# Product operands moved by 64 bytes within each partition of the on-chip memory, in a fused attention, expert and gated-unit kernel

## The chip, the core and the metric

The kernel runs on one core of one Trainium2 chip. Its metric is the device time of one execution in microseconds. Three runs of the kernel before gave 1065.58, 1065.71 and 1065.73 us; the median is 1065.71 us. A core has a matrix engine (TensorE: PE for its matmuls, PEld for its weight loads), a vector engine (VectorE, DVE), a scalar engine (ScalarE, ACT), a third elementwise engine (GpSimd, POOL) and queues for transfers (SP). All of them work on SBUF, a memory of 128 partitions; a tile takes the same byte addresses in each partition. Matmul results go to PSUM, another memory.

## The reference

Three layers follow each other: an attention with a coarse and a local part, a mixture of eight experts with balanced gates, and a gated unit.

```python
x = (out_up + out_local)                       # attention, to 1152 tokens x 512
P = balanced(exp(x @ w_gate))                  # eight rounds of row and column normalisation
for e in range(8):
    out += P[:, e:e+1] * (np.maximum(x @ w1[e], 0.0) @ w2[e])     # w1[e] 512x1024, w2[e] 1024x512
y = ((out @ w_a) * (out @ w_b)) @ w_out        # w_a, w_b 512x1536, w_out 1536x512
```

## The kernel before

Every float32 operand of a large matmul is split into a high part and a low part, and each product is a sum of three matmuls: high by high, high by low, low by high. A matmul instruction has a stationary operand, up to 128 columns that a weight load (LDWEIGHTS) brings into the array, and a moving operand that streams through it. All matmuls go through `mm` (lines 59 and 60): its second argument is the stationary operand, its third the moving one.

The experts' work is cut into 16 units (an expert's half of the hidden width, 512 columns), the gated unit's into six (256 columns). The 1152 tokens are worked on in two chunks, 512 tokens (four tiles of 128) and 640 tokens (five tiles). Units 0 and 1 are worked on in blocks of 384 tokens, before the chunks begin. Each unit has two layers:

- First layer (`g_plain`, `g_chunk`, `g_whole`): the stationary operand is a block of weights from the ring `w` (13 blocks, `new_block`), the moving operand is the activations: `xh` and `xl`, or their combinations `Th` and `Tl`, with 256, 320 or 384 columns. Its results, evicted from PSUM and split, are the product operands `gh` and `gl`.
- Second layer (`o_mm`, line 526): the stationary operand is 128 columns of `gh` or `gl`, the moving operand is a block of second weights from the same ring, 512 columns. A token tile takes 12 matmuls for an expert unit, six for a gated unit. The result is added to `acc`.

Three weight blocks of unit 1's second layer do not lie in the ring but in spare tiles, `we` (line 1301).

The two layers alternate on PE: `phase` (line 825) runs the first layer of one chunk, and puts the second layer's tiles of the other chunk between its steps. The instruction order of each engine is fixed when the program is built.

The place of a tile in a partition comes from the order and sizes of the pools. Pools `const`, `xp`, `gp`, `wr` and `stg` stand one behind the other from below: `P` and small tiles, `xh`, `xl`, a tile `line` that nothing reads or writes (line 86), `acc`, then `gh0`, `gh1`, `gl0`, `gl1` (pool `gp`; used by units 0 and 1, and by chunk 1 afterwards), then the ring, then the staging tiles. From above come `spare`, `tp` (with `Th`, `Tl`, and the unused tile `linet`) and `g0p`, which holds chunk 0's product operands `gh_00`, `gh_01`, `gl_00`, `gl_01` and an unused tile `lineg` (line 1464). Each slice that a matmul reads starts a multiple of 256 bytes behind its tile's start.

The start of these tiles in a partition, modulo 256 bytes, in the built program:

| tiles | read by PE as | start modulo 256 |
|---|---|---|
| `xh`, `xl`, `Th`, `Tl` | moving, first layer | 192 |
| ring blocks `w` | stationary in the first layer, moving in the second | 0 |
| `gh`, `gl` in `gp` (units 0 and 1, chunk 1) | stationary, second layer | 0 |
| `gh_0`, `gl_0` in `g0p` (chunk 0) | stationary, second layer | 0 |
| `we` (three blocks of unit 1) | moving, second layer | 224 |
| `acc` | stationary in transposes; source of the stores to the output | 0 |

Of the kernel before, what the change touches and what calls it, by code (L numbers as in the profile page):

```python
# [8 lines left out]
F32 = mybir.dt.float32  # L9
# [10 lines left out]
def attn_moe_glu_kernel(  # L20
# [42 lines left out]
    xp = ctx.enter_context(tc.tile_pool(name="xp", bufs=1))  # L63
    gp = ctx.enter_context(tc.tile_pool(name="gp", bufs=1))
# [18 lines left out]
    P = P_[:, 0:NT, 0:E]  # L83
    xh = xp.tile([128, KT, N], F32R, name="xh")
    xl = xp.tile([128, KT, N], F32R, name="xl")
    xp.tile([128, 16], F32, name="line")
    acc = [xp.tile([128, DM], F32, name=f"acc{t}") for t in range(NT)]


# [377 lines left out]


    GP = [[gp.tile([128, 4, TB], F32R, tag=f"{x}{n}", name=f"{x}{n}") for n in range(2)] for x in ("gh", "gl")]

    def g_part(u, ps, b, f, kts):

        cols = slice(b * TB, (b + 1) * TB)
        for kt in kts:
            w = u.w[f // 2, kt // 2]
            o = (kt % 2) * 256 + (f % 2) * 128
            a_h, a_l = w.hi[:, o:o + 128], w.lo[:, o:o + 128]
            parts = (a_h, xh), (a_l, xh), (a_h, xl)
            for k, (l, r) in enumerate(parts):
                mm(ps, l, r[:, kt, cols], kt == 0 and k == 0, kt == KT - 1 and k == 2)  # L480
        M.pe += 0.52 * len(kts)
# [24 lines left out]
    def g_plain(u, n, b, f, mid, ps=None, full=False):  # L506

        gh, gl = GP[0][n], GP[1][n]
        if ps is None:
# [31 lines left out]
    def o_moe(u, gh, gl, t, tt, mid=None, first=False):  # L541
        if u.e > 0:
            while gens[0] is not None:
                side_step()
        ps = o_mm(u, gh, gl, t)
        if mid:
            if closed:
                pump(0.0)
            mid()
        if not first:  # L550
            pump()
        a = acc[tt]
        if u.e == 0:
            if u.hf == 0 and closed:
                nc.scalar.copy(out=a, in_=ps)
                act(0.65)
                return
            if u.hf == 0:
                nc.vector.tensor_copy(out=a, in_=ps)
            else:  # L560
                nc.vector.tensor_tensor(out=a, in0=ps, in1=a, op=ALU.add)
        else:
            if u.e == 1 and u.hf == 0:
                nc.scalar.mul(out=a, in_=a, mul=P[:, tt, 0:1])
                act(0.65)
            nc.vector.scalar_tensor_tensor(  # L566
                out=a, in0=ps, scalar=P[:, tt, u.e:u.e + 1], in1=a, op0=ALU.mult, op1=ALU.add
            )
        dve(0.76)
        if first:  # L570
            pump()
# [693 lines left out]
    with tc.manual_schedule():  # L1265
# [134 lines left out]
        for b in range(NB):  # L1400
# [23 lines left out]
            for n in range(2):  # L1424
# [5 lines left out]
                for f in range(4):  # L1430
# [7 lines left out]
                lambda n=n, t=t, b=b: o_moe(  # L1438
                    units[n], *([G[n][:, f] for f in range(4)] for G in GP), t, b * per + t, mid)
                for t in range(per)  # L1440
# [11 lines left out]
        g0p = ctx.enter_context(tc.tile_pool(name="g0p", bufs=1, side="right"))  # L1452
# [8 lines left out]
        for x, G in (("h", GH), ("l", GL)):  # L1461
            t = [g0p.tile([128, 2, 512], F32R, tag=f"g{x}_0{n}", name=f"g{x}_0{n}") for n in range(2)]
            G.append([t[f // 2][:, f % 2] for f in range(4)])
        g0p.tile([128, 48], F32, tag="lineg", name="lineg")

        def o_tile(u, c, t):
            tt = TILES[c][t]
# [112 lines left out]
```

## Time and profile before

| what | value |
|---|---|
| median of three runs | 1065.71 us |
| the profiled execution's own time | 1065.72 us |
| its span, first to last instruction | 1063.9 us |
| PE busy | 1055.9 us (99%) |
| weight loads busy | 964.9 us (91%) |
| VectorE, ScalarE, GpSimd busy | 773.9, 456.9, 521.4 us |
| granted TensorE clock, mean | 1.000 |

The end of a matmul in the trace is modelled and lies behind the start of the next one, so consecutive records overlap. The distance between two starts is the pace at which PE really goes; a record's duration is longer than that by a nearly fixed amount. In the rows below, a name on the left of the arrow is written, those on the right are read; for a matmul the first of these is the moving operand, the second the stationary one, and numbers of buffers are left out (`gh` stands for all tiles of that kind).

### The profile page before, as it was taken

How to read it: one execution, taken by the hardware profiler on the slowest of the kernel's cores; microseconds unless marked ns; L12 is line 12 of the kernel's file. 1: busy time of each engine (PE TensorE's matmuls, PEld its weight loads, DVE VectorE, ACT ScalarE, POOL GpSimd, SP SyncE). 2: the span in 40 equal slices, each digit the busy share in tenths (PEclk: the TensorE clock that was granted, in tenths of full speed). 3: DMA queues.
4: the chain of work that ended last, by engine and by line, in shares of the span. 5: the costliest groups of instructions: out<-in, count | busy, mean ns of one | idle time of the engine just before them, and what ended most of it. 6: DMA issues, size and time to landing. Idle time of an engine off the chain costs nothing.

```text
span 1063.9 us, 17910 instructions
## 1 busy us (share of the span) xinstructions
PE 1055.9 (99%) x6508; PEld 964.9 (91%) x6508; DVE 773.9 (73%) x1535; ACT 456.9 (43%) x1143; POOL 521.4 (49%) x516
## 2 busy tenths in 40 slices
PE   8999999999999999999999999999999999999998
PEld 7999988998899998999999899999989899999997
DVE  7885638777778887877788787778855576667664
ACT  7764514554445344344534434453443553233221
POOL 4532226544655646455564645556451375355521
PEclk9999999999999999999999999999999999999999
DMA  6743001232313233231323223131322002121002
GB/s 166 172 121 96 14 1 40 70 105 65 117 52 127 78 126 95 82 116 54 127 66 128 101 88 106 64 127 58 117 67 60 21 1 60 60 60 42 20 21 89
DMA packets 81256, 84.50 MB, mean 79 GB/s; under 512 B 35856, under 2 KB 55312, under 8 KB 81168
## 3 DMA queue, kind: packets, MB, share of 16 engines
q1 hardware_dynamic: 79984, 83.07, 25.3%
q8 instruction: 51, 0.84, 0.3%
q10 hardware_dynamic: 1184, 0.30, 0.1%
q14 instruction: 37, 0.30, 0.1%
HBM read 71.54 MB, written 11.80 MB: 78 GB/s over the span
## 4 chain that ended last, share of the span: by engine, by line
PE 74%; DVE 0%; issue 0%
PE g L60 73%; PE g L840 0%; DVE acc L1478 0%; DVE G L705 0%
## 5 line engine op out<-in xcount | busy, mean ns | idle before, releaser
L60 PE MATMUL g<-w,gh 128*128 128x512 f32 x1314 | 408.7, 392 | 0.0
L60 PE MATMUL g<-xh,w 128*128 128x256 f32 (+2 forms) x1536 | 333.3, 301 | 0.2 <-DVE G L705 0.2
L701 POOL TENSOR_TENSOR gl<-G,gh 128x256 fp32r<-128x256 f32 (+1 forms) x208 | 172.7, 839 | 265.3 <-ACT gh L699 259.0
L60 PEld LDWEIGHTS g<-w,gh 128*128 128x128 f32 x1314 | 235.7, 188 | 38.0
L60 PEld LDWEIGHTS g<-xh,w 128*128 128x128 f32 x1536 | 255.0, 189 | 4.9 <-DVE G L705 0.6
L60 PE MATMUL g<-w,gl 128*128 128x512 f32 x657 | 256.2, 390 | 0.0
L60 PE MATMUL g<-xl,w 128*128 128x320 f32 (+2 forms) x768 | 230.4, 300 | 0.0
L138 DVE TENSOR_TENSOR w<-raw,w 128x512 fp32r<-128x512 f32 x135 | 127.4, 954 | 108.4 <-ACT w L137 108.3
L60 PE MATMUL g<-Th,w 128*128 128x320 f32 (+1 forms) x912 | 199.0, 295 | 0.2 <-DVE G L705 0.2
L705 DVE TENSOR_TENSOR G<-g,G 128x256 f32<-128x256 f32 (+1 forms) x380 | 154.6, 447 | 24.2 <-PE g L60 9.3
L697 ACT ACTIVATE G<-G 128x256 f32<-128x256 f32 (+1 forms) x168 | 74.3, 443 | 210.7 <-DVE G L705 210.7
L60 PEld LDWEIGHTS g<-Th,w 128*128 128x128 f32 x912 | 152.3, 188 | 4.8 <-DVE G L705 1.9
L60 PEld LDWEIGHTS g<-xl,w 128*128 128x128 f32 x768 | 144.2, 188 | 3.8
L60 PEld LDWEIGHTS g<-w,gl 128*128 128x128 f32 x657 | 123.5, 188 | 26.6
L60 PE MATMUL g<-Tl,w 128*128 128x256 f32 (+1 forms) x456 | 134.2, 294 | 0.0
L566 DVE SCALAR_TENSOR_TENSOR acc<-g,P,acc 128x512 f32<-128x512 f32 x126 | 93.7, 744 | 51.1 <-PE g L60 45.8
L699 ACT CAST gh<-G 128x256 fp32r<-128x256 f32 (+1 forms) x208 | 90.2, 433 | 91.5 <-DVE G L715 78.1
L137 ACT CAST w<-raw 128x512 fp32r<-128x512 f32 x180 | 107.4, 619 | 48.7 <-POOL raw L268 43.6
L398 POOL TENSOR_TENSOR dec<-dec 128x384 f32<-128x384 f32 x48 | 48.7, 1014 | 96.8 <-DVE dec L395 96.8
L60 PEld LDWEIGHTS g<-Tl,w 128*128 128x128 f32 x456 | 85.7, 188 | 2.8
L138 POOL TENSOR_TENSOR w<-raw,w 128x512 fp32r<-128x512 f32 x45 | 59.3, 1324 | 24.0 <-ACT w L137 24.0
L268 POOL TENSOR_TENSOR s<-raw 128x512 f32<-128x512 f32 x38 | 62.2, 1637 | 3.9 <-DMA raw<-w 3.4
(178 smaller groups left out, 1137.8 us busy)
## 6 DMA issues: line engine op xcount, KB each, us to landing
raw<-in_moe_w_dram SPq DMA_DIRECT2D x128, 256.0 KB
w<-dec SPq DMA_DIRECT2D x48, 192.0 KB
dec<-in_moe_w_a_dram SPq DMA_DIRECT2D x16, 384.0 KB
dec<-in_moe_w_b_dram SPq DMA_DIRECT2D x16, 384.0 KB
dec<-in_moe_w_out_dram SPq DMA_DIRECT2D x16, 384.0 KB
raw<-w SPq DMA_DIRECT2D x48, 128.0 KB
raw<-w SPq DMA_DIRECT2D x12, 256.0 KB
vw<-in_v_dram SPq DMA_DIRECT2D x72, 35.0 KB
```

The source lines that it names most:

```text
L60: nc.tensor.matmul(out=o, lhsT=l, rhs=r, start=start, stop=stop, skip_group_check=not check)
L137: nc.scalar.copy(out=hi, in_=raw)
L138: lows.append(lambda: (low or nc.vector).tensor_tensor(out=lo, in0=raw, in1=hi.bitcast(F32), op=ALU.subtract))
L268: nc.gpsimd.tensor_tensor(out=o(), in0=A(*a), in1=A(*b), op=op)
L398: nc.gpsimd.tensor_tensor(out=tf, in0=tf, in1=mf, op=ALU.add)
L566: nc.vector.scalar_tensor_tensor(out=a, in0=ps, scalar=P[:, tt, u.e:u.e + 1], in1=a, op0=ALU.mult, op1=ALU.add)
L697: nc.scalar.activation(out=src, in_=src, func=AF.Relu)
L699: nc.scalar.copy(out=h, in_=src)
L701: nc.gpsimd.tensor_tensor(out=l, in0=src, in1=h.bitcast(F32), op=ALU.subtract)
L705: nc.vector.tensor_tensor(out=o, in0=bank_, in1=b, op=ALU.add)
```

## The change

Two sizes of unused tiles are changed and one unused tile is added. No instruction is added, removed or moved on any engine, and no wait changes; only places of tiles do.

```diff
@@ pool xp, ahead of acc
-    xp.tile([128, 16], F32, name="line")
+    xp.tile([128, 32], F32, name="line")
@@ pool gp, behind GP
+    gp.tile([128, 48], F32, tag="linep", name="linep")
@@ pool g0p, behind gh_0 and gl_0
-        g0p.tile([128, 48], F32, tag="lineg", name="lineg")
+        g0p.tile([128, 32], F32, tag="lineg", name="lineg")
```

What that does to places, in bytes of a partition (from the two built programs):

| tiles | before | after | modulo 256 |
|---|---|---|---|
| `xh`, `xl`, `Th`, `Tl`, `we` | 18880, 37312, 181696, 195520, 217056 | the same | unchanged |
| `acc0` | 55808 | 55872 | 0 to 64 |
| `gh0`, `gh1`, `gl0`, `gl1` | 74240, 80384, 86528, 92672 | 64 higher | 0 to 64 |
| `gh_00`, `gh_01`, `gl_00`, `gl_01` | 165120, 169216, 173312, 177408 | 64 higher | 0 to 64 |
| `w0` to `w12`, staging tiles | 98816 for `w0` | 256 higher | unchanged, 0 |

## Rows read from the trace of the kernel before

**Rows 1.** The page: span, busy time by engine, granted clock in tenths.

```profile
span 1063.9 us, 17910 instructions
...
PE 1055.9 (99%) x6508; PEld 964.9 (91%) x6508; DVE 773.9 (73%) x1535; ACT 456.9 (43%) x1143; POOL 521.4 (49%) x516
...
PEclk9999999999999999999999999999999999999999
```

**Rows 2.** The chain of waits in order of time: start us, us, what.

```profile
276.59 558.32 PE g L60 x3288
...
852.68 207.58 PE g L60 x1332
...
1060.28 0.69 DVE acc L1478
```

**Rows 3.** Groups by shape on PE, whole span: names, shapes, count, busy, mean ns.

```profile
L60 PE MATMUL g<-w,gh 128*128 128x512 f32 x1314 | 408.7, 392 | 0.0
L60 PE MATMUL g<-w,gl 128*128 128x512 f32 x657 | 256.2, 390 | 0.0
L60 PE MATMUL g<-xh,w 128*128 128x320 f32 x672 | 157.5, 309 | 0.0
L60 PE MATMUL g<-xh,w 128*128 128x256 f32 x672 | 130.6, 281 | 0.2 <-DVE G L705 0.2
...
L60 PE MATMUL g<-xl,w 128*128 128x320 f32 x336 | 103.8, 309 | 0.0
L60 PE MATMUL g<-xl,w 128*128 128x256 f32 x336 | 94.2, 280 | 0.0
...
L60 PE MATMUL g<-we,gh 128*128 128x512 f32 x54 | 17.0, 396 | 0.0
...
L60 PE MATMUL g<-we,gl 128*128 128x512 f32 x27 | 10.7, 396 | 0.0
```

**Rows 4.** Timeline, second-layer tile of chunk 1: start us, us, instruction, count.

```profile
602.45 0.62 PE L60 MATMUL g<-w,gh 128*128 128x512 f32 x2
...
602.90 0.39 PE L60 MATMUL g<-w,gl 128*128 128x512 f32 x1
602.91 0.41 PEld L60 LDWEIGHTS g<-w,gh 128*128 128x128 f32 x2
...
603.81 0.28 PE L60 MATMUL g<-xh,w 128*128 128x256 f32 x1
```

**Rows 5.** Timeline, second-layer tile of chunk 0.

```profile
625.28 0.63 PE L60 MATMUL g<-w,gh 128*128 128x512 f32 x2
...
626.44 0.39 PE L60 MATMUL g<-w,gl 128*128 128x512 f32 x1
...
628.04 0.31 PE L60 MATMUL g<-xh,w 128*128 128x320 f32 x1
```

**Rows 6.** Groups by shape on PE, 1054.7 to 1060 us, the last four tiles.

```profile
L60 PE MATMUL g<-w,gh 128*128 128x512 f32 x16 | 4.9, 389 | 0.0
L60 PE MATMUL g<-w,gl 128*128 128x512 f32 x9 | 3.5, 389 | 0.0
```

**Rows 7.** Timeline, first layer with 320 columns.

```profile
628.18 0.31 PE L60 MATMUL g<-xl,w 128*128 128x320 f32 x1
...
629.50 0.31 PE L60 MATMUL g<-xl,w 128*128 128x320 f32 x1
```

**Rows 8.** Timeline, first layer with 256 columns, at the beginning of a phase.

```profile
646.22 0.28 PE L60 MATMUL g<-xl,w 128*128 128x256 f32 x1
...
647.81 0.63 PE L60 MATMUL g<-w,gh 128*128 128x512 f32 x2
```

**Rows 9.** Timeline, first layer with 256 columns, later in a phase.

```profile
608.41 0.28 PE L60 MATMUL g<-xl,w 128*128 128x256 f32 x1
...
609.36 0.39 PE L60 MATMUL g<-w,gh 128*128 128x512 f32 x1
```

## The prediction, made before the changed kernel ran

> **What bounds the kernel now.** I read the page first: PE is busy for 1055.9 of 1063.9 us, and its clock is granted in full in all forty slices, which is the 2.4 GHz level [rows 1]. The chain of waits says the same in order of time: from 276.59 us it is PE's matmuls and nothing else for 558 us, then, after a short mixed piece, for another 208 us, and the last thing in it is a VectorE add at 1060.28 us [rows 2]. So no wait can be won or lost; what counts is the pace of the matmuls themselves. At 2.4 GHz a matmul of n columns would need n/2.4 ns, and the groups by shape with the timeline show how much longer it takes.
>
> The second layer has 1314 + 657 = 1971 matmuls of 512 columns with a ring block moving, recorded with 392 and 390 ns [rows 3]. A record is longer than the pace. In the settled tile of the timeline six matmuls lie between the starts at 602.45 and 603.81 us, so the pace is 1360/6 = 226.7 ns [rows 4]. The last tiles are settled too, and their records have 389 ns [rows 6]; I use 389.5, since tiles in the middle give 389 or 390. Record minus pace is therefore some 163 ns. 512/2.4 is 213.3 ns, so a settled matmul loses 13.4 ns. In the same timeline the next weight load starts with the matmul (602.90 and 602.91 us) [rows 4]: PE reads two operands at a time, the one that streams and the next stationary one. The change moves these two against each other.
>
> Not every tile is settled. A tile of chunk 0 begins with five matmuls between 625.28 and 626.44 us, 232 ns each, and its twelve take 2.76 us, 230 ns each [rows 5]. The mean over all 1971 is (2 x 392 + 390)/3 = 391.3 ns by record, 1.8 ns above settled.
>
> **The change part by part.** Nothing is issued, removed or moved on any engine, and no wait is added, so there is no queue to follow; the three edits only move places, and have one answer. What is left is how fast the same reads go.
>
> *Second layer, 1971 matmuls.* Stationary and moving operand now start at the same place modulo 256 bytes; afterwards the moving one starts 64 bytes below the stationary one. No second-layer row has this relation, but the first layer has it throughout (activations at 192, ring at 0). There, nine matmuls of 320 columns lie between 628.18 and 629.50 us: 146.7 ns each, against 320/2.4 = 133.3, a loss of 13.4 ns [rows 7], and the 1008 matmuls of 320 columns with `xh` and `xl` have a mean of 309 ns over the whole span, like this stretch [rows 3]. So the loss with the new relation is the settled loss of the old one, but without the stretches at 232 ns. If the second layer takes it over, its pace is 213.3 + 13.4 = 226.7 ns everywhere, and the gain is 1.8 ns x 1971 = 3.5 us. With records rounded to 1 ns this is uncertain by about 1 us.
>
> The bounds. Below: with 256 columns the first layer has two paces. At the beginning of a phase 14 matmuls take 1.59 us, 113.6 ns each [rows 8]; later in a phase eight take 0.95 us, 118.8 ns each [rows 9]. Against 106.7 the losses are 6.9 and 12.1 ns. The lightest loss seen is thus some 6.7 ns less than settled; for all 1971 that is 13.2 us more gain, 16.7 us in all. Above: the 81 matmuls whose moving operand is a spare block, 32 bytes below the stationary one modulo 256, are recorded with 396 ns [rows 3], a pace of 233 ns and a loss of 20 ns. If the new relation costs as much, the loss is (396 - 391.3) x 1971 = 9.3 us. I take the value of the 320-column rows, as they are the only long matmuls with the very relation.
>
> *The 81 matmuls with spare blocks* get a relation of 160, which no row shows: 81 x 6.7 ns, 0.5 us either way; I take nothing. *The first weight load of each tile* lies under a first-layer matmul whose relation goes from 192 to 128: 198 tiles (22 units by nine), 1.3 us either way; nothing. *First layer:* the places of its operands don't change against each other, but the pace with 256 columns changes from 114 to 118 ns within a phase, after a second-layer tile. If the quicker pace survives, perhaps 1000 such matmuls (there are 1008 with `xh` and `xl` alone [rows 3]) gain 4 ns, 4 us; if it is never entered, 2 us are lost. I take nothing and widen the range.
>
> *Evictions and transfers.* `acc`, `gh` and `gl` are written by other engines, which do not bound [rows 1]; covered, and even a slowdown of all of them by some ns would stay so. The output's last store is on the end: from the last add's end, 1060.97 us, to the span's end it is 2.9 us [rows 1, 2].
> The Trainium skill, "DMA: Bandwidth & Descriptors", section "How a descriptor splits into AXI transactions", says that a descriptor which does not start at a multiple of 256 bytes fetches from the boundary below it, and the unused bytes cost beats too. It speaks against this change, since `acc` now starts at 64: by it a row of 2048 bytes would need about 66 beats for 64, an estimate from that page of 3%, at most 0.1 us of this tail. No run here shows it yet.
>
> **Sum.** The profiled execution took 1065.72 us, the median 1065.71, so no correction is needed. 1065.7 - 3.5 = 1062.2 us.
>
> **The rivals.** The least difference that a measurement tells is 0.2%, 2.1 us.
>
> 1. *The relation does not matter (1065.7 us).* For it: the settled loss is 13.4 ns with either relation [rows 4, 7], so it may be a fixed cost of each matmul, and the 232 ns stretches may come from the order of what ran before, since they stand at the beginning of a tile. The slower spare blocks start at 224, which is no multiple of 64, so they may be slow for that alone. Against it: two streams that did not touch each other should not have two paces with 256 columns.
> The Trainium skill, "TensorE: Matmul & The Clock Gate", section "Step-by-step: what each phase is for", gives PE two independent read ports in SBUF, one for the moving operand and one for the weights. By that rule this rival holds. The trace bears it out only half: equal losses speak for it, two paces for one shape against it.
>
> 2. *The new relation collides more often (1075 us).* The moving stream starts 64 bytes below the weights and goes through memory faster than these, so it runs into them once more early in every 512-column matmul; a short matmul could be over before the last collision. The price is that of the spare blocks, 233 ns: 1065.7 + 9.3 = 1075.0. For it: the spare blocks also start below, and the slower 256-column pace is found with this relation. Against it: the 320-column matmuls have the relation and lose no more than the settled ones. It decides from a mean record over 392.4 ns on (1.1 ns above now, 2.1 us).
>
> 3. *One collision less (1049 us).* The second layer loses only what the quick 256-column matmuls lose: 1065.7 - 16.7 = 1049.0. For it: that loss exists with this relation. Against it: no longer matmul has it.
>
> **How the numbers follow.** My forecast gets 0.36 (its own range 1060 to 1064.5), rival 1 gets 0.20, rival 2 0.34, rival 3 0.10. Faster by over 0.2% is the forecast nearly whole and rival 3: 0.44. Within 0.2%: rival 1 and an edge of the forecast, 0.21. Slower: rival 2 and an edge of the first-layer term, 0.35. For eight in ten the range leaves out most of rival 3 and the far side of rival 2: 1055 to 1077 us.
>
> **What would show it.** If I am right, the two 512-column groups have 389 or 390 ns, a chunk-0 tile takes 2.72 us, and the 320-column groups still 309 ns. Rival 1 leaves 392 and 390; rival 2 shows some 396; rival 3 about 383. A change in the 256-column groups (281 and 280 ns) would show that the first layer's pace depends on what runs between. The forecast is wrong if the 512-column records rise, or if they fall and the span doesn't. The tail behind the last add should stay at 2.9 us.

## The result and the profile after

The changed kernel takes 1074.72 us (median of four runs, 1074.57 to 1075.97) where the kernel before takes 1065.72 us in the same comparison (1065.58 to 1065.85). The ratio is 1.0086, with a 95% interval of 1.0073 to 1.0098: 9.0 us slower. The forecast was 1062.2 us, so its direction is wrong. The profiled execution is the slowest of the four, 1075.97 us, with a span of 1074.2 us.

The page's head first, to be held against [rows 1]: PE is still busy all the time, its clock is still granted in full.

```profile
span 1074.2 us, 17910 instructions
...
PE 1067.1 (99%) x6508; PEld 966.8 (90%) x6508; DVE 774.8 (72%) x1535; ACT 458.5 (43%) x1143; POOL 521.1 (49%) x516
...
PEclk9999999999999999999999999999999999999999
```

The chain of waits of the changed kernel, in order of time (start us, us, what):

```profile
167.41 676.62 PE g L60 x3938
...
861.92 208.56 PE g L60 x1332
```

PE works through here too; no wait has come in. The last piece has the same 1332 matmuls as in [rows 2] and takes 208.56 us for 207.58. The groups by shape answer to [rows 3]:

```profile
L60 PE MATMUL g<-w,gh 128*128 128x512 f32 x1314 | 413.5, 395 | 0.0
L60 PE MATMUL g<-w,gl 128*128 128x512 f32 x657 | 259.7, 395 | 0.0
L60 PE MATMUL g<-xh,w 128*128 128x320 f32 x672 | 157.7, 309 | 0.0
L60 PE MATMUL g<-xh,w 128*128 128x256 f32 x672 | 129.8, 279 | 0.0
...
L60 PE MATMUL g<-xl,w 128*128 128x256 f32 x336 | 93.7, 279 | 0.0
...
L60 PE MATMUL g<-we,gh 128*128 128x512 f32 x54 | 17.0, 395 | 0.0
```

The 512-column records went from 392 and 390 to 395 ns, about 3.7 ns by record; no other group of the two layers moved by more than 2 ns. The spare blocks did not move, and the ring's matmuls now look like them. The distance between starts says the same more sharply, since a record's end is modelled. This is a tile of chunk 0 in the timeline, at the place of [rows 5]:

```profile
647.25 0.63 PE L60 MATMUL g<-w,gh 128*128 128x512 f32 x2
...
648.65 0.63 PE L60 MATMUL g<-w,gh 128*128 128x512 f32 x2
...
650.05 0.31 PE L60 MATMUL g<-xh,w 128*128 128x320 f32 x1
```

Six matmuls lie between each two of these starts: 1.40 us, 233.3 ns each, and the second six take the same as the first. The tile is settled, but at 233.3 ns and not at the 226.7 of [rows 4]. Taken over all starts of the trace, chunk 0's 816 second-layer matmuls went from a mean of 229.7 to 233.4 ns (+3.0 us), the other 1154 with a successor in the trace from 229.1 to 234.1 (+5.9 us). Together that is 8.9 of the 9.0 us. The profiled execution's span grew by 10.3 us; the further 1.4 us lie mostly in the matmuls outside the two layers, those of the attention and the like (the 784 distances from their starts to the next sum to 89.7 us, for 88.0), and this execution is 1.25 us above the median of the four.

The tail is as it was: the last add starts at 1070.51 us.

```profile
1070.51 0.69 DVE L1480 TENSOR_TENSOR acc<-g,acc 128x512 f32<-128x512 f32 x1 [0.71 <-PE g L60]
```

It ends at 1071.2, and 3.0 us later the span ends, for 2.9 before.

### The profile page after: what moved, and what is told of

Same layout as the page of the kernel before. It is cut to its first block, busy times and chain, and to the rows that moved or that the text cites. A ratio compares the mean times of both kernels' runs of the same rounds, so it can differ in the third digit from the quotient of the medians.

```text
span 1074.2 us, 17910 instructions
## 1 busy us (share of the span) xinstructions
PE 1067.1 (99%) x6508; PEld 966.8 (90%) x6508; DVE 774.8 (72%) x1535; ACT 458.5 (43%) x1143; POOL 521.1 (49%) x516
## 4 chain that ended last, share of the span: by engine, by line
PE 98%; DVE 1%; ACT 0%; issue 0%; DVEq 0%; ACTq 0%
PE g L60 91%; PE at L60 5%; PE at L1061 1%; PE at L938 0%; PE g L842 0%; PE at L1056 0%; PE at L952 0%; ACT p L1031 0%; DVE b L641 0%; ACT pd L1034 0%; PE at L1133 0%; DVE x L1100 0%; DVE acc L1480 0%; ACT od L1091 0%; DVE g L1161 0%
## 5 line engine op out<-in xcount | busy, mean ns | idle before, releaser
L60 PE MATMUL g<-w,gh 128*128 128x512 f32 x1314 | 413.5, 395 | 0.0
L60 PE MATMUL g<-w,gl 128*128 128x512 f32 x657 | 259.7, 395 | 0.0
```

Source lines behind the costliest of these rows:

```text
L60: nc.tensor.matmul(out=o, lhsT=l, rhs=r, start=start, stop=stop, skip_group_check=not check)
```

## The experiments

"Relation" means the start of the moving operand less that of the stationary one, modulo 256 bytes: 0 in the second layer before, -64 after. All mean paces are distances between starts, taken over the whole trace. Unless said otherwise an experiment is an edit of the kernel before, and its ratio is against that kernel on the same chip.

### One part alone, and the same relation at other places

**chunk0_64**: only chunk 0's product operands moved.

```diff
-        g0p.tile([128, 48], F32, tag="lineg", name="lineg")
+        g0p.tile([128, 32], F32, tag="lineg", name="lineg")
```

> Only chunk 0's product operands start at 64 modulo 256; chunk 1's, acc and everything else stay at 0. Theory 1 (what counts is the place of the moving operand against the next stationary one, modulo 256) and theory 2 (what counts is the stationary operand's own place, 64 being a bad one) both expect chunk 0's 816 second-layer matmuls at 233.4 ns as after the change (229.7 before), so +3.0 us, 1068.7 us, and chunk 1's left at 229.1. A third theory, that acc's place or the transfers cost the time, expects 1065.7 us.

Measured: 1069.85 us, ratio 1.0036 (1.0021 to 1.0050). Chunk 0's pace is 233.0 ns, chunk 1's stays at 228.8. So each chunk pays for its own operands. Chunk 0's step is worth 816 x 3.3 ns = 2.7 us; the time is 1.15 us above the 1068.7 expected, and what that is made of is not shown.

**acc_64**: only the accumulators moved.

```diff
-    xp.tile([128, 16], F32, name="line")
+    xp.tile([128, 32], F32, name="line")
     acc = [xp.tile([128, DM], F32, name=f"acc{t}") for t in range(NT)]
+    xp.tile([128, 48], F32, name="linea")
```

> Only the accumulators start at 64 modulo 256; all matmul operands of both layers stay where they were. Theories 1 and 2 expect no change, 1065.7 us within 0.2%, and 512-column records of 392 and 390 ns. The third theory (acc or the stores) expects 1068 to 1075 us.

Measured: 1065.61 us, ratio 0.9998 (0.9989 to 1.0008). The 512-column groups of this run:

```profile
L60 PE MATMUL g<-w,gh 128*128 128x512 f32 x1314 | 408.4, 392 | 0.0
L60 PE MATMUL g<-w,gl 128*128 128x512 f32 x657 | 255.9, 390 | 0.0
```

They are those of the kernel before. The accumulators' place and with it the output's stores cost nothing that can be seen: the third theory falls.
The Trainium skill, "DMA: Bandwidth & Descriptors", section "How a descriptor splits into AXI transactions", would have the stores from 64 modulo 256 cost some more beats; the run agrees with the estimate of at most 0.1 us in that it shows no cost, and it cannot show one so small.

**all_down_64**: the changed kernel's relations with the product operands at 0 as before. Activations go to 128, the ring to 192.

```diff
+    const.tile([128, 48], F32, name="linec")
-    xp.tile([128, 16], F32, name="line")
+    xp.tile([128, 32], F32, name="line")
+    gp.tile([128, 48], F32, tag="linep", name="linep")
-            tp.tile([128, 8], F32, name="linet")
+            tp.tile([128, 24], F32, name="linet")
-        g0p.tile([128, 48], F32, tag="lineg", name="lineg")
+        g0p.tile([128, 32], F32, tag="lineg", name="lineg")
```

> The changed kernel's relations at other places: activations at 128, ring at 192, product operands at 0, so that in both layers the moving operand starts 64 below the stationary one, as in the changed kernel, but the product operands have the place that they had before. Theory 1 expects the changed kernel's time, 1074.7 us, and second-layer records of 395 ns. Theory 2 (the stationary operand's own place, 64) expects the second layer as before, 392 and 390 ns, 1065.7 us.

Measured: 1074.49 us, ratio 1.0084 (1.0069 to 1.0099), the changed kernel's time. Its 512-column groups, and six matmuls of one tile:

```profile
L60 PE MATMUL g<-w,gh 128*128 128x512 f32 x1314 | 413.5, 395 | 0.0
L60 PE MATMUL g<-w,gl 128*128 128x512 f32 x657 | 259.7, 395 | 0.0
```

```profile
647.19 0.63 PE L60 MATMUL g<-w,gh 128*128 128x512 f32 x2
...
648.59 0.63 PE L60 MATMUL g<-w,gh 128*128 128x512 f32 x2
```

The busy times and means of these two groups are the changed kernel's to the digit, and the six take 1.40 us again, with the product operands where the kernel before had them. Theory 2 falls: it is the relation.

### Other relations in the second layer

**c1_128_c0_192** and **c1_192_c0_128** give the chunks two further relations and then change them over. The edit sets `line`, `linep` and `lineg` so that the operands start at the places named; here that of the first:

```diff
-    xp.tile([128, 16], F32, name="line")
+    xp.tile([128, 48], F32, name="line")
+    gp.tile([128, 32], F32, tag="linep", name="linep")
-        g0p.tile([128, 48], F32, tag="lineg", name="lineg")
```

> Two other relations in one run: chunk 1's product operands at 128 (moving operand 128 below), chunk 0's at 192 (moving operand 64 above), ring at 0. Theory 1 expects paces that depend on the relation and between 227 and 240 ns, a different one in each chunk, with no figure from before for either; by the picture that a stream which starts below runs into the weights and one that starts above has passed them, chunk 0 should have 227 ns or less and chunk 1 some 233. Theory 2 leaves 128 and 192 open. If the relation does not matter at all, both have 229 ns and the time is 1065.7 us.

> The two chunks' relations of an earlier run changed over: chunk 1's product operands at 192 (moving operand 64 above), chunk 0's at 128 (128 below). If the relation alone sets the pace, chunk 1 now has about 230.6 ns and chunk 0 about 232.8, and the time is 1065.7 + 1154 x 1.5 ns + 816 x 3.1 ns = 1070 us. If the chunk (its phases, its neighbours) sets it, chunk 1 keeps 232.8 and chunk 0 230.6.

Measured: 1069.45 us (1.0035, 1.0022 to 1.0048) and 1071.58 us (1.0053, 1.0038 to 1.0068). With +64 chunk 0 has 230.6 and chunk 1 231.9 ns, with 128 chunk 1 has 232.8 and chunk 0 231.7. Neither expected outcome of the exchange came: between these two relations a chunk's pace differs by 0.9 or 1.0 ns, and between the two chunks, at the same relation, by 1.1 or 1.2. So the relation alone does not set the pace; the chunk, with the matmuls that run before its tiles, counts as much here. A moving operand that starts above costs too, so the picture of a stream that runs into the weights only when it starts below is not borne out: it expected 227 ns or less.

**c1_32_c0_224** asks what makes the spare blocks slow.

```diff
-    xp.tile([128, 16], F32, name="line")
+    xp.tile([128, 24], F32, name="line")
+    gp.tile([128, 56], F32, tag="linep", name="linep")
-        g0p.tile([128, 48], F32, tag="lineg", name="lineg")
+        g0p.tile([128, 56], F32, tag="lineg", name="lineg")
```

> Second layer only: chunk 1's product operands at 32 (moving operand 32 below), chunk 0's at 224 (moving operand 32 above). If the spare blocks are slow for their relation (32 below), chunk 1 has 233 ns like them, +5 us; if they are slow because their own start is no multiple of 64, chunk 1 stays near 227 to 229 ns. Chunk 0 has no row to go by: between 227 and 233 ns, 1065 to 1069 us for it alone.

Measured: 1070.57 us, ratio 1.0044 (1.0029 to 1.0059). Chunk 1 with -32 has 234.1 ns, chunk 0 with +32 has 232.7. The moving operand now starts at a multiple of 64 and is as slow as the spare blocks, so these are not slow for the moving operand's own place. But the stationary operands start at 32 and 224 here, so this run does not exclude that any 512-column matmul with one operand off a multiple of 64 is slow; no run tried both operands off it with the relation 0. With 320 columns such a place of the moving operand costs nothing that can be seen (x_224 and x_160 below).

The second layer lost 8.3 us by its paces, the time only some 4.7: the first layer's 256-column matmuls, whose own relation stayed at -64, went from a mean of 117.0 to 115.1 ns, 3.3 us less. This is the sign that the prediction named for a first layer whose pace depends on what runs between.

### Other relations in the first layer

**x_same** gives the first layer the relation 0, **x_above_64** +64, **x_224** -32 and **x_160** -96; the second layer stays as before. The edit is an unused tile ahead of `xh` and other sizes of `line`, `linet` and `lineg`; x_same:

```diff
+    const.tile([128, 16], F32, name="linec")
-    xp.tile([128, 16], F32, name="line")
-            tp.tile([128, 8], F32, name="linet")
+            tp.tile([128, 56], F32, name="linet")
-        g0p.tile([128, 48], F32, tag="lineg", name="lineg")
```

> The first layer's activations and their combinations start at 0 modulo 256 like the ring, so that the first layer has the relation that the second had before the change; the second layer is as before the change. Theory A (as in the prediction: with one relation each matmul loses a fixed time, whatever its columns): the 320-column matmuls keep 146.7 ns, the 256-column ones 117, and the time is 1065.7 us. Theory B (with one relation the loss is a share of the columns, some 10% where the moving operand starts 64 below and 6.3% where both start at one place, so the first layer's 13.4 ns could not be carried over to 512 columns): 320 columns at 141.7 ns, 256 at 113.3, 1692 x (5.2 + 3.7) ns = 15 us less, 1051 us.

> The first layer's moving operands start 64 above the ring's blocks modulo 256 instead of 64 below; the second layer is as before the change. Theory A: 1065.7 us. Theory B gives a share of its own to this relation; from chunk 0's 230.6 ns with 512 columns and the moving operand 64 above (8.1%), 320 columns take some 144 ns and 256 some 115, 1692 x (2.7 + 2) = 8 us less, 1058 us.

> First layer's moving operands 32 below the ring instead of 64 below, second layer as before the change. Theory C: 320 columns keep 146.7 ns (as with three other relations), 256 columns settle at a whole number of steps: at one step (113.3 ns) the time falls by 1692 x 3.7 ns = 6 us to 1059.5, at two (120 ns) it rises by 5 us to 1070.7. Theory that an operand which starts at no multiple of 64 costs one step more: 320 at 153.3 and 256 at 120, 1082 us.

> First layer's moving operands 96 below the ring, second layer as before the change. The same two outcomes as with 32 below: 256 columns at one step, 1059.5 us, or at two, 1070.7 us, with 320 columns at 146.7 ns; an extra step for operands off a multiple of 64 would give 1082 us.

Measured: x_same 1071.60 us (1.0053, 1.0038 to 1.0068), x_above_64 1070.69 (1.0044, 1.0027 to 1.0061), x_224 1068.53 (1.0020, 1.0011 to 1.0029), x_160 1069.53 (1.0030, 1.0018 to 1.0041). No theory hit these times. The groups of x_same:

```profile
L60 PE MATMUL g<-xh,w 128*128 128x320 f32 x672 | 157.4, 309 | 0.0
L60 PE MATMUL g<-xh,w 128*128 128x256 f32 x672 | 133.3, 283 | 0.0
```

and a stretch of it with 256 columns:

```profile
601.34 0.40 PE L60 MATMUL g<-xh,w 128*128 128x256 f32 x2
...
602.06 0.28 PE L60 MATMUL g<-xh,w 128*128 128x256 f32 x1
```

Six matmuls take 0.72 us, 120 ns each, steadily: 13.3 ns over 106.7. With relation 0, matmuls of 256 and 512 columns settle at the same loss, and 320 columns have it in the mean. Theory B (a share of the columns) falls. But 320 columns have that loss with every relation that was tried, while 256 and 512 columns differ:

| relation | 256 columns | 320 columns | 512 columns, chunk 0 / chunk 1 |
|---|---|---|---|
| 0 | 119.8 | 146.6 | 229.7 / 229.1 |
| -64 | 117.0 | 146.9 | 233.4 / 234.1 |
| +64 | 118.3 | 146.7 | 230.6 / 231.9 |
| -32 | 118.6 | 147.1 | chunk 1: 234.1 |
| +32 | not tried | not tried | chunk 0: 232.7 |
| -96 | 119.1 | 147.0 | not tried |
| 128 | not tried | not tried | 231.7 / 232.8 |

(mean ns from start to start; the first two columns over 1692 matmuls each, from x_same, the kernel before, x_above_64, x_224 and x_160.)

The neighbours count too. In these four runs the second layer was left at relation 0, and its paces still moved: chunk 0 had 229.2, 230.6, 227.2 and 228.4 ns in x_same, x_above_64, x_224 and x_160, chunk 1 230.8, 231.2, 230.6 and 230.0 (before: 229.7 and 229.1). So differences of some 2 ns between rows can come from what runs before; the 3.7 and 5.0 ns of the change are larger.

### Fewer columns, and one part of the operand alone

**cols_before** and **cols_after** leave out columns in the chunks' second layers, at the places of the two kernels.

```diff
+    cols = [512]
...
+                n = 512 if k == 0 else cols[0]
-                mm(ps, l, r, k == 0, k == 3 * u.no - 1)
+                mm(ps[:, :n], l, r[:, :n], k == 0, k == 3 * u.no - 1)
...
+            cols[0] = (448, 384)[c]
```

> The same with fewer columns at the places of the kernel before (both operands at one place): 448 columns in chunk 0, 384 in chunk 1, the other columns' sums left out. Theory C: with this relation the loss is two steps, 13.3 ns, whatever the columns (as 256 and 320 columns showed when the first layer got this relation): 173.3 and 200.0 ns settled. Theory B (6.3% of the columns): 170 and 198.4 ns.

> Places as in the changed kernel (moving operand 64 below). In the second layer of the chunks all matmuls but the first of a tile leave out columns: 448 instead of 512 in chunk 0, 384 in chunk 1, so the sums of the left-out columns are not formed. Theory C (a settled matmul loses whole steps of 6.67 ns, and with this relation the number of steps grows with its columns: one to two at 256, two at 320, three at 512): 384 columns take 173.3 ns (two steps) or 180.0 (three), 448 take 200.0 or 206.7, with 448 at three. Theory B (a share of the columns, 9.4 to 10%): 176 and 205 ns. Theory A (a fixed loss): 13.4 ns in each case would contradict the 233 ns at 512.

Measured, one profile each: with 384 columns the mean pace is 173.9 ns at relation 0 and 174.8 at -64; with 448 columns 203.1 and 202.0 (over distances under 260 ns, which leaves out waits). Their times, 1038.46 and 1041.11 us, hold waits for weights as well and are not used. At relation 0 a tile with 384 columns settles at theory C's figure:

```profile
605.70 0.51 PE L60 MATMUL g<-w,gh 128*128 128x384 f32 x2
...
606.74 0.51 PE L60 MATMUL g<-w,gh 128*128 128x384 f32 x2
```

Six in 1.04 us are 173.3 ns, two steps of 6.67 over 160. But 448 columns never settle at 200, and with the relation -64 they are no slower than with 0. Theory C is right that many settled losses are whole steps (113.3, 120.0, 173.3, 226.7, 233.3 ns), and wrong that the number of steps grows with the columns: with 320, 384 and 448 columns the two relations differ by about 1 ns at most.

Nor is it a rule for every matmul. In the kernel before, the stretch whose end [rows 9] shows begins here:

```profile
607.94 0.28 PE L60 MATMUL g<-xh,w 128*128 128x256 f32 x1
```

Twelve matmuls up to 609.36 us take 1.414 us by the starts in ns, 117.8 each: a steady loss of 11.1 ns, five steps in three matmuls. This is the commonest pace of 256 columns in that kernel. In the changed kernel most tiles of chunk 1 alternate between 231 and 236 ns and have 233.3 only in the mean.

**low_64** and **high_64** move one part of the product operands; here the edit of low_64, shortened.

```diff
-    GP = [[gp.tile(... tag=f"{x}{n}" ...) for n in range(2)] for x in ("gh", "gl")]
+    GP = [[gp.tile(... tag=f"gh{n}" ...) for n in range(2)]]
+    gp.tile([128, 16], F32, tag="linel", name="linel")
+    GP.append([gp.tile(... tag=f"gl{n}" ...) for n in range(2)])
+    gp.tile([128, 48], F32, tag="linep", name="linep")
...
+            if x == "l":
+                g0p.tile([128, 16], F32, tag="linel0", name="linel0")
...
-        g0p.tile([128, 48], F32, tag="lineg", name="lineg")
+        g0p.tile([128, 32], F32, tag="lineg", name="lineg")
```

> Only the low parts gl of the product operands start at 64 modulo 256, the high parts gh stay at 0 (both chunks). A tile's matmuls come in threes: gh with w's high part, gh with its low part, gl with the high part. Theory next (the running matmul collides with the weight load of the next one): the second of each three, which runs while gl is loaded, takes 233 ns, the others 227. Theory own (it collides with its own stationary operand's place): the third takes 233 ns. Either way one matmul in three is slow: 1065.7 + 1971/3 x 4.6 ns = 1068.7 us. Theory phase (a settled pace belongs to a whole run of equal relations): no such pattern of three, and some time between 1066 and 1075 us.

> Only the high parts gh start at 64, the low parts gl at 0, acc at 64 (which cost nothing by itself). Theory next: the first and third of each three take 233 ns, the second 227, 1065.7 + 2 x 1971/3 x 4.6 ns = 1071.7 us. Theory own: the first and second. Theory phase: no such pattern, between 1066 and 1075 us; the sum of what this run and the one with only the low parts add need not be the change's 9 us.

Measured: 1068.92 us (1.0026, 1.0017 to 1.0036) and 1072.92 us (1.0063, 1.0048 to 1.0078). The times are near those of theories next and own, the places only in part. In low_64 a settled three in chunk 0 takes 228, 229 and 236 ns: the slow one is the third, which rules out theory next, and theory phase too, as it expected no pattern of three. This is such a tile:

```profile
637.92 0.61 PE L60 MATMUL g<-w,gh 128*128 128x512 f32 x2
...
639.31 0.62 PE L60 MATMUL g<-w,gh 128*128 128x512 f32 x2
...
640.69 0.31 PE L60 MATMUL g<-Th,w 128*128 128x320 f32 x1
```

Twelve matmuls take 2.77 us, a three 693 ns: two steps more than the 680 of the kernel before. Theory own would give one step. In high_64 two settled threes take 233, 233, 236, 235, 229 and 234 ns, 1400 in all: three steps more for each three, as when both parts are moved. Two and three don't add up to three, and own's fast third is missing. What one matmul loses depends on its neighbours.

**th_224**: only `Th` and `Tl` moved, in search of a quicker version.

```diff
-            tp.tile([128, 8], F32, name="linet")
-        g0p.tile([128, 48], F32, tag="lineg", name="lineg")
+        g0p.tile([128, 56], F32, tag="lineg", name="lineg")
```

> Only the combinations Th and Tl start at 224 (32 below the ring), all else as before the change. When all first-layer operands stood at 224, chunk 0's second-layer tiles were settled from the start (227.2 ns for 229.7, 2 us less), but the 256-column matmuls and chunk 1's tiles lost 4.5 us. If Th alone brings the settled tiles, 1064 to 1065 us and a version quicker than both; if it brings the loss too, 1066 to 1068 us.

Measured: 1067.28 us, ratio 1.0011 (1.0002 to 1.0020). Chunk 0's tiles gain, 228.3 ns for 229.7, and chunk 1's (230.0) and the 256-column matmuls (117.7) lose a little more. No placing that was run beats the kernel before.

## Why the prediction was wrong, point by point

**What bounds the kernel** was right: the chain is PE's, the clock is full, and in the profiled executions the second layer's pace adds 8.9 us, where the medians differ by 9.0.

**"So the loss with the new relation is the settled loss of the old one, but without the stretches at 232 ns"** is the step that failed. It took the 320-column matmuls for the sum because they had the very relation [rows 7]. They have 146.6 to 147.1 ns with five relations, so their row says nothing about any of them. It was the wrong row, and one that could have been doubted: in the same trace, with the same relation, 256 columns lost 6.9 and 12.1 ns [rows 8, 9] (11.1 by the starts in ns), so the loss was no property of the relation alone. The half that came true is that the stretches vanish in chunk 0: its tiles settle, but a step higher, at 233.3 ns where the prediction had 226.7. Instead of 3.5 us gained, 8.9 were lost.

**The bound above** was the answer. It came from the spare blocks, the only 512-column matmuls in the trace with another relation than 0: 396 ns, a loss of 9.3 us. The measured records have 395, the time 9.0 us. c1_32_c0_224 shows that it was not the moving operand's start off a multiple of 64 that made them slow. The columns should have been matched ahead of the relation. That the fit is so close is partly luck: the blocks lie 32 below and the change puts the ring 64 below, and nothing in the trace before said that both cost the same (234.1 ns in chunk 1 with either); 64 above and 128 cost less.

**Rival 1**, no effect, falls by all_down_64 and chunk0_64.
The Trainium skill's two independent read ports ("TensorE: Matmul & The Clock Gate", section "Step-by-step: what each phase is for") would have made it true. The measurement differs, by 0.86%, and decides: the pace depends on how the two operands lie to each other, so their reads are not free of each other here. How they meet is not shown.

**Rival 2** had the price, 1075.0 us, and the record, 396 ns. Its mechanism is not shown. That 320, 384 and 448 columns lose no more with -64 than with 0, within some 1 ns, would suit it. But starting above costs as well (230.6 and 231.9 ns with +64), and 256 columns are slower with 0.

**Rival 3** did not happen; no run of 512-column matmuls settled under two steps.

**What was taken at nothing.** The accumulators and the stores: right (acc_64). The spare blocks: right, 395 and 398 ns. The first layer: its 256-column mean went from 117.0 to 116.8 ns, 0.5 us gained, inside what was left for it. c1_32_c0_224 shows that this term can be larger, 3.3 us.

**The range** of 1055 to 1077 us holds 1074.72; the forecast, and the 0.44 for faster against 0.35 for slower, leaned the wrong way.

**What stays open.** That the relation costs the time is shown, and so are the settled losses. How PE's two reads meet, so that 512 columns take a third step with -64 and 256 columns fewer with -64 than with 0, is not. It may be that with 256 and 512 columns each matmul begins in the same phase of the two streams as the one before it, and the relation picks that phase, while with 320 it wanders and gives the mean. The steady 120.0 ns, chunk 0's 233.3 and the changing 145 to 150 ns of 320 columns fit this, and so do the sums of low_64 and high_64; the alternating 231 and 236 ns of chunk 1 and the steady 173.3 ns of 384 columns do not follow from it, and no run shows it.

## What to carry to other kernels

When PE is the bound, the places of the moving and the stationary operand against each other are worth about 1% here, and the best relation of those tried belongs to a shape: 0 for 512 columns, -64 for 256, none for 320. The matmuls that run before shift the pace as well, so a new placing is measured in the whole kernel. A price is carried only from rows with the same shape; a row that has the new property but another shape must first be shown to answer to that property. Unused tiles of 32 to 224 bytes are enough to try it, with nothing else in the program moved.

## What the runs showed of the hardware that was not expected

- Settled paces of this kernel lose whole steps of 6.67 ns over columns/2.4 GHz, the time in which 16 columns, 64 bytes, stream: one (113.3 ns with 256 columns), two (120.0, 173.3, 226.7 ns with 256, 384, 512; 146.7 with 320 in the mean) or three (233.3 ns with 512). Where not each matmul does, several together can: 256 columns with -64 lose five steps in three matmuls (117.8 ns each), low_64's threes eight.
- It is the relation modulo 256 that costs here, not the place: with the operands elsewhere and the same relations, the 512-column groups agree to the tenth of a microsecond (413.5 and 259.7 us).
- A pace depends on what ran before, also where its own relation stays: with 512 columns at relation 0 chunk 0 has 227.2 to 230.6 ns, by the first layer's relation, and 256 columns at -64 have 117.0 or 115.1, by the second layer's. The chunk-0 tile of [rows 5] begins with five matmuls at 232 ns; the changed kernel's tile above has 233.3 from its first.
